# Attention and two expert layers in one kernel: the hidden layer at another SBUF offset, and weights converted 1024 columns at a time

## The chip, the cores and the metric

The kernel runs on one core of a Trainium2 chip. The metric is the device time of one execution in microseconds (us). Before the change three executions took 1100.30, 1100.47 and 1101.81 us; the median is 1100.47 us.

## What is computed

Three stages follow each other, all in float32 at the boundary:

```python
scores = q @ k.T / 8                       # 4 batches x 8 heads, 576 rows, 64 columns
mask: row block i // 64 may see column blocks j // 64 <= i // 64
x = softmax(scores) @ v                    # laid out as 2304 tokens x 512
x = ((x @ w1) * (x @ w2)) @ w3 @ w_out     # 512 -> 1024 -> 1024 -> 512
logits = x @ w_gate + log1p(exp(x @ w_noise)) * noise
top2, softmax over the two chosen logits
out[token] += weight * (relu(x[token] @ w1[e]) @ w2[e])    # 8 experts, 1024 hidden columns
```

## The kernel before

**Numbers in two parts.** A float32 matrix is split by `split` (L472) into a rounded high part (a copy to `fp32r` on ScalarE) and a low part (a subtraction on VectorE, or on GpSimd where `low="pool"`). `mm3` (L482) then makes three TensorE products: high by high (L485), high by low (L486), low by high (L487).

**Attention, heads 0 to 31.** `prep_h` (L604) makes the two parts of q and k of a head: `hi` on ScalarE (L607, L610), q's low part on VectorE (L609), and `kl`, k's low part, on GpSimd (L612). `s_unit` (L622) makes the scores, `s_max` (L645) the row maxima `nm` on VectorE (L653) and the exponentials on ScalarE (L658), `g_unit` (L661) transposes them on TensorE into `pt`, and `av_a` and `av_b` multiply by v. Heads 0 to 7 keep `pt` whole in two buffers; from head 8 on `pt` has both parts.

**Weights of the first layer.** They arrive as 64-bit words that VectorE takes apart. `load64` (L536) loads 128 x 512 words (512 KB) into one of two buffers `stg`; `conv64` (L541) makes 512 float32 columns `stf` of them with three VectorE instructions (L547, L548, L549), and `feed_half` (L764) splits `stf` into a weight tile `pc`: ScalarE L476, VectorE L480. There are 40 such jobs; a load is issued when the job two places ahead of it has been taken apart. When eight of them are there, TensorE makes the product w3 @ w_out in 64 units (`w_unit`, L717, tile `m<-pc,pc`) beside the heads.

**First layer.** For nine chunks of 256 tokens `ab` (L199) makes x @ w1 and x @ w2 (tile `m<-xh,pc`), their product `gt` in two parts, and `yout` (L215) multiplies `gt` by the product w3 @ w_out (tile `m<-pc,gt`: `gt` is TensorE's stationary operand, `pc` the moving one of 512 columns). The router's small steps follow.

**Experts.** `trans` (L930) transposes gathered tokens into `xt`, `ffn1` (L944) makes the hidden layer `ht` from `xt` and `pc`, and `ffn2` (L959) multiplies `ht`, stationary, by `pc`, moving, 512 columns (tile `ph<-pc,ht`). An expert has 640 rows: 384 in part 0 (`xt0`, `ht0`) and 256 in part 1 (`xt1`, `ht1`).

**Order.** The strings FIRST and LATER (L70, L71) list what is written out for one head: `g`, `p`, `s`, `a`, `b`, `h` are the steps of attention, `f` gives TensorE so many us of other matmuls, and `c` is one call of `feed`, which splits the job before and takes the next one apart. A scheduler then places the instructions on each engine by priorities (PIECE_PRIO, W_PRIO, MOE_PRIO). All loads and stores named here are issued by SyncE, in one queue.

**Places in SBUF.** In the built program the tiles stand at these byte offsets modulo 512: all twelve `pc` at 128, `gt` at 384, `xh` and `yT` at 384, `xt0` at 352, `xt1` at 448, `ht0` at 416, `ht1` at 448, `pt` of heads 0 to 7 at 128 and of the later heads at 480.

Of the kernel before, what the change touches and what calls it, by code (L numbers as in the profile page):

```python
# [22 lines left out]
P = 128  # L23
# [43 lines left out]

FIRST = "g0 g1 t f2.9 c t c o g2 g3 t p s0 t t s1 s2 f2.9 c t a f2.9 t b0 t s3 h t t c c b1 v l"  # L70
LATER = "g0 g1 f2.6 o g2 p t c g3 t t t s0 s1 s2 t c t a f2.6 s3 b0 t t c f2.6 c t b1 h v l"  # L71


# [8 lines left out]
class Moe1:  # L82


    def __init__(self, k, p2, psM):
        self.k, self.tc, self.nc, self.a, self.p2 = k, k.tc, k.nc, k.a, p2
        self.psM = self.psR = psM
        self.p2s = ExitStack()
        self.ready, self.rt, self.ticks, self.conv = 0, iter(()), 1, 0
        self.xs, self.gts, self.ys, self.lg = {}, {}, {}, {}  # L90
        self.scat, self.marks = [], ()

    def setup_load(self):
        nc, a, p2 = self.nc, self.a, self.p2
# [134 lines left out]
    def logits_t(self, c, t):  # L229
        nc, p2 = self.nc, self.p2  # L230
        y = self.ys[c, t]
        px = self.psR.tile([P, 4, P], F32, name="m")
        for d in range(4):
            nc.tensor.transpose(px[:, d, :], y[:, d * P:(d + 1) * P], self.k.ident)
        if t == 0:
            self.yT = self.p2b.tile([P, 2, 4, CH], F32R, name="yT")
        self.k.split([self.yT[:, i, :, t * P:(t + 1) * P] for i in range(2)], px)

    def logits_m(self, c):
# [224 lines left out]
class Kernel:  # L464
# [69 lines left out]
        return [(tab[:, b * P:e * P].rearrange("e (p i) -> p e i", p=P), ids[:, :, b:e]) for b, e in ((0, NA), (NA, NSLOT))]  # L534

    def load64(self, src, n):  # L536
        t = self.stg.tile([P, 512], I64, name="stg")
        self.nc.sync.dma_start(t.rearrange("p (a b) -> p a b", a=n), src)
        return t

    def conv64(self, t):  # L541

        v = self.nc.vector
        wi = t.bitcast(I32).rearrange("p (n w) -> p n w", w=2)
        f = self.stg.tile([P, 512], F32, name="stf")
        fi = f.bitcast(I32)
        v.tensor_scalar(fi, wi[:, :, 1], 0x07FFFFFF, 3, op0=OP.bitwise_and, op1=OP.logical_shift_left)  # L547
        v.scalar_tensor_tensor(fi, wi[:, :, 1], -0x40000000, fi, op0=OP.bitwise_and, op1=OP.bitwise_or)  # L548
        v.scalar_tensor_tensor(fi, wi[:, :, 0], 29, fi, op0=OP.logical_shift_right, op1=OP.bitwise_or)  # L549
        return f  # L550


    def attention(self):
        tc, nc, a = self.tc, self.nc, self.a
        moe1 = self.moe1
        with tc.tile_pool(name="p1", bufs=1, side="right") as p1, tc.tile_pool(name="stg", bufs=2, side="right") as self.stg, \
                tc.tile_pool(name="psS", bufs=3, space=PSUM) as psS, \
                tc.tile_pool(name="psT", bufs=2, space=PSUM) as psT, \
                tc.tile_pool(name="psV", bufs=1, space=PSUM) as psV:
# [4 lines left out]
            nc.vector.tensor_copy(mkl, mk32[:, 0, :])  # L564
            nc.vector.tensor_copy(mkr, mk32[:, 1, 0:64])
            sums = p1.tile([P, B, 6, H], F32, name="sums")

            hd = {}
            pxs = ExitStack()
# [34 lines left out]
            def prep_h(h):  # L604
                c = hd[h]
                c.hi = buf(h, [P, 2, S], F32R, "hi")
                nc.scalar.activation(c.hi[:, 0, :], c.qk[:, 0, :], AF.Copy, scale=0.125)  # L607
                lo = c.hi[64:128, 0, :]
                nc.vector.scalar_tensor_tensor(lo, c.qk[64:128, 0, :], 0.125, r32(lo), op0=OP.mult, op1=OP.subtract)  # L609
                nc.scalar.copy(c.hi[:, 1, :], c.qk[:, 1, :])  # L610
                c.kl = buf(h, [P, S], F32R, "kl")
                nc.gpsimd.tensor_tensor(c.kl, c.qk[:, 1, :], r32(c.hi[:, 1, :]), op=OP.subtract)  # L612

            def prep_v(h):
                c = hd[h]
# [45 lines left out]
            def g_unit(h, g):  # L661
                c = hd[h]
                pb = pbs[h < H and h % 2]
                if g == 0:
                    if h < H:
                        c.pt = px.tile([P, 1, PTW], F32, name="pt", bufs=2)
                    else:
                        c.pt = p1.tile([P, 2, PTW], F32R, name="pt")
                base, skip, items = G_UNITS[g]
                bank = psT.tile([P, 512], F32, name="tp")  # L670
                for n, (t, kt) in enumerate(items):
                    nc.tensor.transpose(bank[:, n * P:(n + 1) * P], pb[t][:, kt * P:(kt + 1) * P], self.ident)  # L672
                o = len(items) * P - skip
                src = bank[:, skip:skip + o]
                h_ = c.pt[:, 0, base:base + o]
                nc.scalar.copy(h_, src)
                if h >= H:
                    nc.vector.tensor_tensor(c.pt[:, 1, base:base + o], src, r32(h_), op=OP.subtract)
# [55 lines left out]
            def w_jobs():  # L734

                def wout(g):
                    return a["w_out"][:, g:g + 1, :], 1, g // 2, (g % 2) * 512, 0

                def w3(ft, o):
                    return a["w3"][ft, :, o:o + 512].unsqueeze(1), 1, 4 + ft % 2, o, 0 if ft < 2 else max(16, 8 * (ft - 1))  # L740

                for half in range(2):
                    for ft in range(2):
                        yield w3(ft, half * 512)
                    for g in range(4 * half, 4 * half + 4):
                        yield wout(g)
                for ft in range(2, 8):
                    for o in (0, 512):
                        yield w3(ft, o)
                for m, (n, k, i) in enumerate(W12):  # L750
                    for o in (0, 2):
                        yield a[n][:, o:o + 2, k * 256:(k + 1) * 256], 2, i, o * 256, 0 if m < 2 else 64

            jobs = list(w_jobs())
            raw = []
# [6 lines left out]
                    feed_half()  # L762

            def feed_half():  # L764
                if len(conv) > moe1.conv:
                    _, _, i, o, _ = jobs[moe1.conv]
                    pc = self.pc[i]
                    self.split((pc[:, 0, o:o + 512], pc[:, 1, o:o + 512]), conv[-1], low="dve")
                    moe1.conv += 1
                n = len(conv)  # L770
                if n < len(jobs) and wst.get("n", 0) >= jobs[n][4]:
                    conv.append(self.conv64(raw[n]))
                    if n + 2 < len(jobs):
                        raw.append(self.load64(*jobs[n + 2][:2]))
# [78 lines left out]
            for i in range(-1, BH):  # L853
                if i == 2:
                    moe1.setup_load()
                elif i == 3:
                    moe1.setup()
                elif i == H:
                    pxs.close()
                    moe1.p2b = moe1.p2s.enter_context(tc.tile_pool(name="p2b", bufs=1, reuse_waits="tile"))  # L860
                for op in (FIRST if i < NF else LATER).split():
                    step(i, i + 1, op)
            sums_out(B - 1)
# [65 lines left out]

    def trans(self, e, s):  # L930
        nc, n = self.nc, len(self.part(s))
        x = self.xt[e, s] = (self.pa if s == 0 else self.pb).tile([P, 2, 4, n * P], F32R, name=f"xt{s}")
        wv = self.wv[e, s] = self.pa.tile([P, n], F32, name=f"wv{s}", bufs=2)
        for o, i in enumerate(self.part(s)):
            xg = self.xg[e, i]
            nc.gpsimd.tensor_copy(wv[:, o:o + 1], xg[:, DM + e:DM + e + 1])
# [170 lines left out]
```

## Time and profile before

| what | value |
|---|---|
| median of 3 runs | 1100.47 us |
| the profiled execution, its own time | 1103.1 us |
| its span, first to last instruction | 1101.2 us |
| TensorE matmul (PE) busy | 1050.4 us, 95% |
| TensorE weight load (PEld) busy | 941.2 us, 85% |
| VectorE (DVE) busy | 564.4 us, 51% |
| ScalarE (ACT) busy | 494.9 us, 45% |
| GpSimd (POOL) busy | 309.3 us, 28% |
| bytes moved | 136.34 MB, mean 124 GB/s |
| mean granted TensorE clock | 0.988 of 2.4 GHz |

The profile is of one execution. Busy time is the union of an engine's recorded instructions; successive instructions of VectorE and of TensorE overlap in the records, so the distance from one start to the next tells more of their pace than the duration of one. "Idle before" is the time an engine stood still before an instruction, with what ended it.

### The profile page before, as it was taken

What the parts mean: (1) busy time and instruction counts of PE and PEld (TensorE: products, weight loads), DVE (VectorE), ACT (ScalarE), POOL (GpSimd) and SP (SyncE); (2) the same over time, 40 slices, a digit from 0 to 9 for tenths busy, and PEclk for the clock granted to TensorE, in tenths of its full rate; (3) what the DMA queues carried; (4) which work ended last, traced back from release to release, by engine and by line L of the source; (5) the groups of instructions that cost most, each with busy time, mean ns of one, the idle gap of its engine ahead of it and who ended that gap; (6) DMA issues with size and microseconds to landing.
All of it is one profiled execution on the core that took longest, in us unless ns stands there. A gap on an engine that the chain in (4) does not pass through costs nothing.

```text
span 1101.2 us, 17515 instructions
## 1 busy us (share of the span) xinstructions
PE 1050.4 (95%) x6588; PEld 941.2 (85%) x6588; DVE 564.4 (51%) x1270; ACT 494.9 (45%) x1180; POOL 309.3 (28%) x315
## 2 busy tenths in 40 slices
PE   4999978999999999999999999999999999999996
PEld 3767767799899999989999889889898989899885
DVE  5988889856665756532454453534333333434111
ACT  5765547666665656422223432433333333333111
POOL 3110122424252242422443325241413222120211
PEclk9999989999999999999999999999999999999999
DMA  9765775325634463322413556563545445351212
GB/s 218 237 199 193 196 200 180 123 79 132 196 96 105 143 156 121 107 68 59 77 40 87 126 106 184 173 163 96 148 102 144 107 125 125 106 115 30 39 20 32
DMA packets 80386, 136.34 MB, mean 124 GB/s; under 512 B 21437, under 2 KB 46757, under 8 KB 80293
## 3 DMA queue, kind: packets, MB, share of 16 engines
q1 hardware_dynamic: 70181, 113.98, 36.4%
q0 software_dynamic: 10112, 21.16, 10.7%
q8 instruction: 54, 0.88, 0.3%
q14 instruction: 39, 0.32, 0.1%
HBM read 103.92 MB, written 31.19 MB: 123 GB/s over the span
## 4 chain that ended last, share of the span: by engine, by line
PE 81%; DMA 8%; DVE 7%; ACT 1%; issue 1%; SPq 1%; POOL 0%; POOLq 0%; DVEq 0%; ACTq 0%
PE ph L485 13%; PE ph L486 13%; PE ph L487 13%; PE m L485 9%; PE m L486 9%; PE m L487 9%; DMA stg<-in_w_dram 4%; PE tp L672 4%; PE av L697 3%; PE sb L642 2%; PE sb L639 2%; PE m L939 1%; DVE stf L549 1%; DVE nm L653 1%; DMA stf<-in_m_dram 1%
## 5 line engine op out<-in xcount | busy, mean ns | idle before, releaser
L485 PE MATMUL m<-xh,pc 128*128 128x256 f32 x576 | 165.2, 290 | 5.6 <-DVE at L211 3.5
L486 PE MATMUL m<-xh,pc 128*128 128x256 f32 x576 | 163.1, 287 | 2.2 <-DVE xh L480 2.2
L487 PE MATMUL m<-xh,pc 128*128 128x256 f32 x576 | 161.2, 287 | 1.9 <-DVE pc L480 1.9
L485 PE MATMUL ph<-xt,pc 128*128 128x384 f32 (+1 forms) x512 | 156.0, 308 | 2.9 <-ACT xt L476 1.6
L486 PE MATMUL ph<-xt,pc 128*128 128x384 f32 (+1 forms) x512 | 157.0, 307 | 0.0
L487 PE MATMUL ph<-xt,pc 128*128 128x384 f32 (+1 forms) x512 | 156.9, 307 | 0.0
L954 DVE SCALAR_TENSOR_TENSOR ht<-ph,ht 128x384 fp32r<-128x384 f32 (+1 forms) x128 | 61.6, 489 | 148.7 <-ACT ht L953 143.5
L480 DVE TENSOR_TENSOR pc<-stf,pc 128x1024 fp32r<-128x1024 f32 (+1 forms) x92 | 92.3, 1016 | 87.2 <-ACT pc L476 83.8
L485 PE MATMUL ph<-pc,ht 128*128 128x512 f32 x320 | 127.8, 400 | 0.0
L486 PE MATMUL ph<-pc,ht 128*128 128x512 f32 x320 | 126.5, 396 | 0.0
L487 PE MATMUL ph<-pc,ht 128*128 128x512 f32 x320 | 126.4, 395 | 0.0
L981 POOL DMA_INDIRECT out_dram<-yo,ids x40 | 64.3, 1606 | 211.5 <-ACT yo L977 124.0
L485 PEld LDWEIGHTS m<-xh,pc 128*128 128x128 f32 x576 | 110.5, 193 | 7.2 <-DVE at L211 3.7
L953 ACT ACTIVATE ht<-ph 128x384 fp32r<-128x384 f32 (+1 forms) x128 | 55.0, 437 | 133.8 <-PE ph L487 127.1
L486 PEld LDWEIGHTS m<-xh,pc 128*128 128x128 f32 x576 | 110.3, 193 | 3.0 <-DVE xh L480 2.6
L487 PEld LDWEIGHTS m<-xh,pc 128*128 128x128 f32 x576 | 109.0, 192 | 2.7 <-DVE pc L480 2.4
L476 ACT CAST pc<-stf 128x1024 fp32r<-128x1024 f32 (+1 forms) x92 | 78.1, 864 | 73.8 <-DVE stf L549 32.5
L658 ACT ACTIVATE pb<-sb,nm 128x288 f32<-128x288 f32 (+3 forms) x192 | 93.5, 496 | 38.4 <-PE tp L672 17.3
L480 POOL TENSOR_TENSOR gt<-at,gt 128x256 fp32r<-128x256 f32 x72 | 57.2, 798 | 183.9 <-ACT gt L476 175.7
L485 PEld LDWEIGHTS ph<-xt,pc 128*128 128x128 f32 x512 | 95.7, 188 | 4.0 <-ACT xt L476 2.1
L612 POOL TENSOR_TENSOR kl<-qk,hi 128x576 fp32r<-128x576 f32 x32 | 47.5, 1484 | 177.2 <-ACT hi L610 136.6
L486 PEld LDWEIGHTS ph<-xt,pc 128*128 128x128 f32 x512 | 96.2, 188 | 0.6 <-DVE xt L480 0.2
(158 smaller groups left out, 2229.0 us busy)
## 6 DMA issues: line engine op xcount, KB each, us to landing
stf<-in_m_dram SPq DMA_DIRECT2D x52, 512.0 KB
qk<-in_qk_dram SPq DMA_DIRECT2D x32, 576.0 KB
stg<-in_w_dram SPq DMA_DIRECT2D x32, 512.0 KB
x<-ev SPq DMA_DIRECT2D x32, 288.0 KB
xab<-x SPq DMA_DIRECT2D x20, 256.0 KB
yt<-y SPq DMA_DIRECT2D x18, 260.0 KB
stg<-in_w_out_dram SPq DMA_DIRECT2D x8, 512.0 KB
v<-in_v_dram SPq DMA_DIRECT2D x24, 160.0 KB
```

The lines of the kernel that those rows point to most:

```text
L476: d = nc.scalar.copy(h, src)
L480: return d, eng.tensor_tensor(l, src, r32(h), op=OP.subtract)
L485: nc.tensor.matmul(out, a, c, start=first, stop=False)
L486: nc.tensor.matmul(out, a, d, start=False, stop=False)
L487: nc.tensor.matmul(out, b, c, start=False, stop=last)
L612: nc.gpsimd.tensor_tensor(c.kl, c.qk[:, 1, :], r32(c.hi[:, 1, :]), op=OP.subtract)
L658: nc.scalar.activation(pb[t][:, k0:k0 + src.free_size()], src, AF.Exp, bias=nm, scale=1.0, accum_out=sums[:, h // H, t + n, h % H:h % H + 1])
L672: nc.tensor.transpose(bank[:, n * P:(n + 1) * P], pb[t][:, kt * P:(kt + 1) * P], self.ident)
L697: nc.tensor.matmul(c.av[:, o0:o0 + w], c.vv[:, kt, :], c.pt[:, i, s0:s0 + w], start=(kt == 0 and i == 0), stop=(kt == 4 and i == m - 1))
L953: a = nc.scalar.activation(hh[:, 0, f, :], ph, AF.Relu)
L954: v = nc.vector.scalar_tensor_tensor(hh[:, 1, f, :], ph, 0.0, r32(hh[:, 0, f, :]), op0=OP.max, op1=OP.subtract)
L981: nc.gpsimd.indirect_dma_start(out=self.a["out"], out_offset=self.idx(e, i), in_=yo, in_offset=None, compute_op=OP.add)
```

## The change

It does three things.

1. In `trans` the tile `xt1` becomes 112 float32 longer, and the weights `wv` of part 0 and 1 become tiles of their own for even and odd experts in place of two buffers of one tile. In the built program `ht0` and `ht1` then both stand at 384 modulo 512 bytes; `xt0`, `xt1`, `pc` and `gt` stay where they were.
2. All jobs of the weights but six become 1024 columns wide (1 MB a load): w3 from its third block on, six of the eight blocks of w_out in pairs, and all of w1 and w2. 23 jobs are left, 17 of them wide. `stg` has two buffers of 1024 words; room for it comes from `pt` of heads 0 to 7, which moves into the tile that the later heads' `pt` uses (now at 320 modulo 512), and from `yT`, which is taken from a new pool that opens when all jobs are done. FIRST has three `c` in place of five.
3. `kl` of heads 0 to 8 is made on VectorE; from head 9 on it stays on GpSimd.

```diff
-FIRST = "g0 g1 t f2.9 c t c o g2 g3 t p s0 t t s1 s2 f2.9 c t a f2.9 t b0 t s3 h t t c c b1 v l"
+FIRST = "g0 g1 t f2.9 c t o g2 g3 t p s0 t t s1 s2 f2.9 c t a f2.9 t b0 t s3 h t t c b1 v l"
...
-            self.yT = self.p2b.tile([P, 2, 4, CH], F32R, name="yT")
+            self.yT = self.p2c.tile([P, 2, 4, CH], F32R, name="yT")
...
     def load64(self, src, n):
-        t = self.stg.tile([P, 512], I64, name="stg")
+        w = n * src.shape[-1]
+        t = self.stg.tile([P, 1024], I64, name="stg", bufs=2)[:, 0:w]
...
-        f = self.stg.tile([P, 512], F32, name="stf")
+        f = self.stg.tile([P, 1024], F32, name="stf")[:, 0:wi.shape[1]]
...
+            pt0 = p1.tile([P, 2, PTW], F32, name="pt")
+            self.stg = stgs.enter_context(tc.tile_pool(name="stg", bufs=1, side="right"))
...
-                nc.gpsimd.tensor_tensor(c.kl, c.qk[:, 1, :], r32(c.hi[:, 1, :]), op=OP.subtract)
+                (nc.vector if h < NF - 1 else nc.gpsimd).tensor_tensor(c.kl, c.qk[:, 1, :], r32(c.hi[:, 1, :]), op=OP.subtract)
...
-                        c.pt = px.tile([P, 1, PTW], F32, name="pt", bufs=2)
+                        c.pt = pt0[:, h % 2:h % 2 + 1, :]
...
+                def wout2(g):
+                    return a["w_out"][:, g:g + 2, :], 2, g // 2, 0, 0
...
-                    for g in range(4 * half, 4 * half + 4):
-                        yield wout(g)
+                    if half == 0:
+                        for g in range(2):
+                            yield wout(g)
+                    for g in range(2 + 2 * half, 4 + 4 * half, 2):
+                        yield wout2(g)
                 for ft in range(2, 8):
-                    for o in (0, 512):
-                        yield w3(ft, o)
+                    yield w3(ft, 0, 1024)
                 for m, (n, k, i) in enumerate(W12):
-                    for o in (0, 2):
-                        yield a[n][:, o:o + 2, k * 256:(k + 1) * 256], 2, i, o * 256, 0 if m < 2 else 64
+                    yield a[n][:, :, k * 256:(k + 1) * 256], 4, i, 0, 0 if m < 2 else 64
...
+                if i >= H and moe1.p2c is None and moe1.conv == 40:
+                    stgs.close()
+                    moe1.p2c = moe1.p2s.enter_context(tc.tile_pool(name="p2c", bufs=1, reuse_waits="tile"))
...
-        x = self.xt[e, s] = (self.pa if s == 0 else self.pb).tile([P, 2, 4, n * P], F32R, name=f"xt{s}")
-        wv = self.wv[e, s] = self.pa.tile([P, n], F32, name=f"wv{s}", bufs=2)
+        x = (self.pa if s == 0 else self.pb).tile([P, 8 * n * P + 112 * s], F32R, name=f"xt{s}")
+        x = self.xt[e, s] = x[:, 0:8 * n * P].rearrange("p (m d c) -> p m d c", m=2, d=4)
+        wv = self.wv[e, s] = self.pa.tile([P, n], F32, name=f"wv{s}{e % 2}")
```

The scheduler's order moves with it. On VectorE, around heads 2 and 3, the program before has these instructions (`hi`: low part of q; `nm`: row maxima; `stf<-stg`: taking apart; `pc<-stf`: low part of a weight tile):

```order
L609 SCALAR_TENSOR_TENSOR hi<-qk,hi 64x576
L480 TENSOR_TENSOR pc_67<-stf,pc_67 128x512
L653 TENSOR_REDUCE nm_482<-sb 128x1
L547 TENSOR_SCALAR stf<-stg 128x512
L548 SCALAR_TENSOR_TENSOR stf<-stg,stf 128x512
L653 TENSOR_REDUCE nm_489<-sb 128x1
L653 TENSOR_REDUCE nm_542<-sb 128x1
L549 SCALAR_TENSOR_TENSOR stf<-stg,stf 128x512
L547 TENSOR_SCALAR stf<-stg 128x512
L548 SCALAR_TENSOR_TENSOR stf<-stg,stf 128x512
L480 TENSOR_TENSOR pc_68<-stf,pc_68 128x512
```

The changed program has there, on the same engine:

```order
L481 TENSOR_TENSOR pc_67<-stf,pc_67 128x512
L549 TENSOR_SCALAR stf<-stg 128x1024
L550 SCALAR_TENSOR_TENSOR stf<-stg,stf 128x1024
L658 TENSOR_REDUCE nm_474<-sb 128x1
L692 COPY ev<-tp 128x128
L614 SCALAR_TENSOR_TENSOR hi<-qk,hi 64x576
L551 SCALAR_TENSOR_TENSOR stf<-stg,stf 128x1024
L661 TENSOR_REDUCE nm_474<-nm_474 128x1
L617 TENSOR_TENSOR kl<-qk,hi 128x576
L658 TENSOR_REDUCE nm_557<-sb 128x1
L658 TENSOR_REDUCE nm_559<-sb 128x1
L481 TENSOR_TENSOR pc_68<-stf,pc_68 128x1024
```

One wide job takes the place of two, and `kl` stands in VectorE's queue between them. SyncE's queue, where the first chunk's rows `xab` and `xr` of the first layer are fetched, has before:

```order
L538 DMA stg<-in_w_dram 128x2x256 x2
L701 DMA x_61<-ev 128x576
L167 DMA xab<-x_61 64x3x256 x2
L172 DMA xr<-rs 64x3x256
L167 DMA xab<-x_61 64x3x256 x2
L538 DMA stg<-in_w_dram 128x2x256
L172 DMA xr<-rs 64x3x256
L538 DMA stg<-in_w_dram 128x2x256
```

and in the changed program:

```order
L540 DMA stg<-in_w_dram 128x4x256
L706 DMA x_61<-ev 128x576
L168 DMA xab<-x_61 64x3x256 x2
L173 DMA xr<-rs 64x3x256
L168 DMA xab<-x_61 64x3x256 x2
L173 DMA xr<-rs 64x3x256
L540 DMA stg<-in_w_dram 128x4x256
```

The two loads among the fetches, each of which waits for a buffer, have become one behind them.

## Rows read from the trace of the kernel before

**Rows 1.** The page: the span.

```profile
span 1101.2 us, 17515 instructions
```

**Rows 2.** Busy us of each engine by stretch, then granted clock, DMA share, GB/s.

```profile
0.00:38.70 38.70, 24.48 (x111) 18.21 (x111) 26.08 (x50) 22.31 (x58) 10.66 (x26) 1.00 0.95 240
38.70:72.00 33.30, 30.68 (x164) 22.48 (x162) 29.98 (x60) 24.83 (x69) 4.82 (x4) 0.95 0.70 217
72.00:119.50 47.50, 45.99 (x244) 35.80 (x242) 41.79 (x83) 28.53 (x76) 4.28 (x3) 1.00 0.53 172
119.50:163.90 44.40, 35.07 (x220) 30.72 (x217) 35.76 (x66) 21.15 (x53) 9.99 (x8) 0.92 0.79 206
163.90:203.40 39.50, 32.83 (x204) 28.47 (x205) 38.55 (x72) 25.78 (x73) 13.01 (x10) 0.89 0.51 165
203.40:620.00 416.60, 413.61 (x2977) 384.62 (x2976) 227.67 (x671) 208.06 (x580) 149.95 (x151) 1.00 0.41 107
620.00:1101.20 481.20, 467.77 (x2680) 420.87 (x2679) 164.54 (x274) 164.28 (x276) 116.54 (x114) 0.99 0.44 107
```

**Rows 3.** TensorE in order of time, experts: start, us, instruction (`ph<-pc,ht` is `ffn2`).

```profile
735.42 0.40 PE L485 MATMUL ph<-pc,ht 128*128 128x512 f32 x1
...
746.63 0.34 PE L485 MATMUL ph<-xt,pc 128*128 128x384 f32 x1
```

**Rows 4.** TensorE in order of time, first layer (`m<-pc,gt` is `yout`).

```profile
464.65 0.40 PE L485 MATMUL m<-pc,gt 128*128 128x512 f32 x1
...
469.88 0.39 PE L487 MATMUL m<-pc,gt 128*128 128x512 f32 x1
```

**Rows 5.** Groups by line and shape: count, busy us, mean ns, idle before.

```profile
L485 PE MATMUL ph<-pc,ht 128*128 128x512 f32 x320 | 127.8, 400 | 0.0
L480 DVE TENSOR_TENSOR pc<-stf,pc 128x1024 fp32r<-128x1024 f32 x52 | 62.5, 1223 | 86.8 <-ACT pc L476 83.7 <-PE ph L487 3.1
L612 POOL TENSOR_TENSOR kl<-qk,hi 128x576 fp32r<-128x576 f32 x32 | 47.5, 1484 | 177.2 <-ACT hi L610 136.6 <-PE m L234 23.0 <-PE av L697 16.7
```

**Rows 6.** VectorE in order of time, heads 0 to 6.

```profile
7.78 1.52 DVE L547 TENSOR_SCALAR stf<-stg 128x512 int32<-128x512 int32 x1
50.89 1.83 DVE L548 SCALAR_TENSOR_TENSOR stf<-stg,stf 128x512 int32<-128x512 int32 x1
56.02 0.67 DVE L548 SCALAR_TENSOR_TENSOR stf<-stg,stf 128x512 int32<-128x512 int32 x1
56.62 0.67 DVE L480 TENSOR_TENSOR pc<-stf,pc 128x512 fp32r<-128x512 f32 x1
72.17 1.54 DVE L547 TENSOR_SCALAR stf<-stg 128x512 int32<-128x512 int32 x1
```

**Rows 7.** GpSimd in order of time, heads 4 and 5.

```profile
50.74 1.43 POOL L612 TENSOR_TENSOR kl<-qk,hi 128x576 fp32r<-128x576 f32 x1 [9.51 <-ACT hi L610]
```

**Rows 8.** Tile `stg`: ns min/median/max, first and last start; what ended VectorE's idle time.

```profile
L547 DVE TENSOR_SCALAR stf<-stg x40: 406/424/1544, 7.8 to 203.8; 128x512 int32<-128x512 int32 x40
DMA stg<-in_w_dram: 14.9, 11
DMA stg<-in_w_out_dram: 2.7, 3
```

**Rows 9.** The chain that ended last, up to 260 us: start, us, what.

```profile
127.24 5.54 DMA stg<-in_w_dram
132.80 4.10 DMA xr<-rs
145.02 9.55 DMA stg<-in_w_dram
```

**Rows 10.** Tiles `yT` and `vz`: first and last start.

```profile
L476 ACT CAST yT<-m x18: 577/587/605, 234.1 to 622.2; 128x512 fp32r<-128x512 f32 x18
L697 PE MATMUL av<-pt,vz x80: 272/434/954, 24.5 to 119.0; 128*128 128x448 f32 x32, 128*128 128x320 f32 x16, 128*128 128x192 f32 x16, 128*128 128x128 f32 x16
```

More of the change, by code (lines that the diff above doesn't have):

```diff
@@ L91, in __init__ @@
         self.scat, self.marks = [], ()
+        self.p2c = None
     def setup_load(self):
@@ L555, in attention @@
         moe1 = self.moe1
-        with tc.tile_pool(name="p1", bufs=1, side="right") as p1, tc.tile_pool(name="stg", bufs=2, side="right") as self.stg, \
+        stgs = ExitStack()
+        with tc.tile_pool(name="p1", bufs=1, side="right") as p1, \
                 tc.tile_pool(name="psS", bufs=3, space=PSUM) as psS, \
@@ L737, in wout, with w3 @@
                     return a["w_out"][:, g:g + 1, :], 1, g // 2, (g % 2) * 512, 0
-                def w3(ft, o):
-                    return a["w3"][ft, :, o:o + 512].unsqueeze(1), 1, 4 + ft % 2, o, 0 if ft < 2 else max(16, 8 * (ft - 1))
+                def wout2(g):
+                    return a["w_out"][:, g:g + 2, :], 2, g // 2, 0, 0
+                def w3(ft, o, w=512):
+                    return a["w3"][ft, :, o:o + w].unsqueeze(1), 1, 4 + ft % 2, o, 0 if ft < 2 else max(16, 8 * (ft - 1))
                 for half in range(2):
@@ L764, in feed_half @@
             def feed_half():
[L765 to L769, printed above, removed]
+                if len(conv) > wst.get("split", 0):
+                    _, _, i, o, _ = jobs[len(conv) - 1]
+                    pc, w = self.pc[i], conv[-1].shape[-1]
+                    self.split((pc[:, 0, o:o + w], pc[:, 1, o:o + w]), conv[-1], low="dve")
+                    wst["split"] = len(conv)
+                    moe1.conv += w // 512
                 n = len(conv)
```

## Prediction

> **What bounds the kernel now.** I read first the span [rows 1] and then the busy time of the engines by stretch [rows 2]. The reader should see two kernels in one. From 203.4 us on TensorE is busy all the time at full clock: up to 620 us it idles 3 of 416.6 us, and from 620 us to the end 468 of 481 us. Nothing that VectorE, GpSimd or the loads save there can shorten the time; only matmuls that follow each other at a smaller distance can. Up to 203.4 us it is otherwise. The first 38.7 us belong to the DMA engines, 0.95 busy at 240 GB/s. From 38.7 to 72 us VectorE is busy 30.0 of 33.3 us. From 72 to 119.5 us TensorE leaves only 1.5 us of 47.5. From 119.5 to 163.9 us nobody is full: TensorE idles 9.3 us at a mean granted clock of 0.92 (some of it at 1.2 GHz, the lower of its two levels, the rest at 2.4), and VectorE 8.6 us. From 163.9 to 203.4 us VectorE is busy 38.55 of 39.5 us and TensorE idles 6.7 us at a clock of 0.89.
>
> Then the distances of matmuls in order of time. In the experts 48 matmuls of the hidden layer `ht1` by `pc`, 512 columns each, lie between 735.42 and 746.63 us [rows 3]: 11.21 / 48 = 233.5 ns each. In the first layer 23 matmuls of `gt` by `pc`, also 512 columns, lie between 464.65 and 469.88 us [rows 4]: 5.23 / 23 = 227.4 ns. The clock is full in both stretches [rows 2], the moving operand is the same kind of tile at 128 modulo 512 bytes, and the stationary one stands at 384 in the faster group and at 448 in the slower.
>
> Last, what VectorE does before 203 us: the tile `stg`, the chain of waits and single instructions [rows 6, 8, 9]. It stood still 17.6 us (14.9 + 2.7, in 14 waits) for loads of `stg` [rows 8], and some of its instructions took over a us longer than their like while GpSimd made `kl`: 1.83 us from 50.89 us where the same instruction takes 0.67 us, beside a `kl` of 1.43 us from 50.74 us [rows 6, 7].
>
> **Part 1, the hidden layer at 384.** `ffn2` has three lines of 320 matmuls, 960 in all [rows 5]. If their distance becomes that of `gt`, the saving is 960 x (233.5 - 227.4) = 5.9 us, all on the path, since TensorE is the bound there [rows 2]. The bounds: 0 from below if the offset does not matter; from above 960 x 7 = 6.7 us, 7 ns being the most that I would read into the same two groups. A loss would need 384 to be worse than 416 or 448 for a stationary operand, against which [rows 4] speaks. I take 5.9 us. The tiles `wv` and the shifted buffers behind `xt1` cost no instruction.
>
> The Trainium skill, "TensorE: Matmul & The Clock Gate", section on the back-to-back issue gap, gives the start-to-start distance of a warm matmul as its columns at 2.4 GHz plus 2.5 ns, 215.7 ns at 512, with no term for where an operand stands; by it this part would bring nothing. Both groups of this trace lie above that, and differ from each other, which the formula does not provide for.
>
> **Part 2, wide jobs.** Recorded durations overlap, so I count pitch: 512 columns take 56.62 - 56.02 = 0.60 us from start to start [rows 6]. From 0.67 us [rows 6] to 1.22 us at 1024 columns [rows 5] each further column costs (1.223 - 0.67) / 512 = 1.08 ns, 0.55 us for 512, so that 0.05 us of the pitch is fixed. A wide job saves four of these on VectorE, 0.2 us; 17 wide jobs 3.4 us. By the recorded durations it would be 2 x 0.67 - 1.22 = 0.12 us each, 8.2 us. I take the pitch, because on a full queue the next instruction starts inside the record of the one before.
>
> The loads change more. A load can start when the job two places ahead is taken apart. The 40 jobs start between 7.8 and 203.8 us [rows 8], one in 5 us, so a load has two paces less its predecessor's own work of some 3 us, about 7 us, to land. Loads of 512 KB landed after 5.54 us, and after 9.55 us where the first layer's rows were fetched [rows 9], hence the waits. With 1 MB the pace is 10 us and the room about 14 us. A 1 MB load lands after 5.5 us if the bytes go in parallel and 11.1 us if they double; both fit. The waits of 17.6 us should go but for the first and some of the crowded ones; 0 to 17.6 us are the bounds on VectorE. On SyncE 17 load issues fewer stand in the queue, and at the first chunk one 1 MB load follows the fetches where two loads stood between them.
>
> **Part 3, `kl` on VectorE.** Nine instructions of 576 columns, by the pitch 0.60 + 64 x 1.08 ns = 0.67 us each: 6.0 us more. Against it stand the stalls beside GpSimd: seven VectorE instructions were stretched beside a `kl` of heads 0 to 8, the first at 7.78 us (1.52 for 0.42 us), the last at 72.17 us (1.54) [rows 6, 8], 7.1 us over the usual in all. Taken together -1.1 us. GpSimd's 9 x 1.43 us had no one waiting long.
>
> **What of it lies on the path.** By stretch [rows 2]. *0 to 38.7 us*: the same bytes, 0. *38.7 to 72 us*: VectorE gets four `kl` (+2.7), loses three stalls (-3.1), two wide jobs' fixed time (-0.4) and some 2 us of waits; TensorE's idle time there is 2.6 us and its clock 0.95. I take -2.5 us. *72 to 119.5 us*: TensorE leaves 1.5 us; -1. *119.5 to 163.9 us*: this holds the longest wait, which ended the load of 9.55 us; VectorE's 8.6 us are nearly all waits for loads, but the first chunk's chain of fetch (4.10 us [rows 9]), sum, product and split stays: -4. *163.9 to 203.4 us*: VectorE is the bound, four wide jobs save 0.8 to 2 us: -1.5. Sum -9 us, between 0 and -18.
>
> **What comes with it.** `yT` in a pool that waits for the last job: first written at 234.1 us [rows 10], the last job's first instruction was at 203.8 us [rows 8]; covered by 30 us, and if the jobs became that late it would cost the lateness. The shared `pt`: head 8 must wait until head 7's last product, whose matmul starts at 119.0 us [rows 10], has been made; the cover is what VectorE and ScalarE do meanwhile, and without it one wait of about 2 us. `pt` at another offset: 240 matmuls, by the difference of 6.1 ns found above at most 1.5 us either way; 0 taken.
>
> **Sum.** Against the profiled execution's 1103.1 us: 1103.1 - 5.9 - 9 = 1088.2 us. Its own time lies 2.6 us above the median of the runs, 1100.47, so for a run without the profiler I forecast 1100.5 - 14.9 = 1085.6 us, rounded to 1086.
>
> **Rivals.**
> - *Only the offset pays*, 0.16. The front stays as long as it is because attention's own chain and the first chunk's fetches set its pace, not VectorE. For it: TensorE leaves only 1.5 us between 72 and 119.5 us, and 4.10 us of the chain are `xr`. Against: VectorE is at 38.55 of 39.5 us in the last stretch. 1100.5 - 5.9 = 1094.6 us.
> - *Only the conversion pays*, 0.11. The 6 ns are due to something else in which the two groups differ (the PSUM tiles, what other engines write meanwhile). For it: only one pair of groups shows it. Against: `gt` keeps 227 ns while VectorE and ScalarE are at work. 1100.5 - 9 = 1091.5 us. The Trainium skill's formula above leads to this case.
> - *Neither pays, or the change doesn't do what it says*, 0.04: 1100.5 us.
> - *Slower, by `kl` behind wide instructions*, 0.05. VectorE runs in order; `kl` now stands behind up to one instruction of 1.22 us, where GpSimd began it at once. If the scores' second half waits for `kl` in each of nine heads, that is 9 x (0.67 + 1.22) = 17 us on the attention path with nothing saved in front: 1100.5 - 5.9 + 17 = 1111.6 us. It decides from the point where `kl` is made less than about 2 us before its scores. Against it: `kl` is made for a head further on, while GpSimd's slower `kl` was idle before it for 9.51 us [rows 7].
>
> **How the numbers follow.** The forecast, both parts paying, has 0.64. With the front between -3 and -16 us and part 1 between 5 and 6.7 us it spans 1078 to 1093 us. The two single cases reach to 1095; a little beyond, 1097, takes in the small waits named above. Below 1078 and above 1097 I leave some 2 in 10. About 0.2% (2.2 us) is what a measurement of this kernel can tell from no change. Faster by more: 0.64 + 0.16 + 0.11 = 0.91; within it 0.04; slower 0.05.
>
> **What would show it.** `ffn2` at 227 ns in every expert, and 5.9 us less from 620 us to the end. VectorE's waits for `stg` down from 17.6 us to a few, no instruction of 1.5 us beside `kl` in heads 0 to 8, and the last job taken apart about 9 us before 203.8 us; TensorE's clock nearer to 1.00 between 119.5 and 203.4 us. Wrong would be: `ffn2` still at 233 ns; the front as long as before with VectorE idle and the fetches of the first chunk ending the waits; or scores of heads 0 to 8 waiting for VectorE's `kl`.

## The result and the profile after

| kernel | median us (range, runs) | ratio to before, 95% interval |
|---|---|---|
| before | 1101.0 (1100.3 to 1101.81, 4) | |
| changed | 1091.7 (1090.7 to 1094.5, 4) | 0.9917 [0.9902, 0.9932] |
| changed, once more | 1092.43 (1089.96 to 1093.77, 6) | 0.9912 [0.9891, 0.9933] |

The change is worth 9.3 us; 14.9 were forecast. The page of the changed kernel gives its span; the profiled execution itself took 1094.5 us and was the slowest of the four.

```profile
span 1092.7 us, 17405 instructions
```

The windows of the changed kernel, with the columns of [rows 2]. They are cut where the first scores of heads 3, 6, 9, 11, 14 and 15 start, as [rows 2] were for heads 3, 6, 9, 11 and 14; the last cut lies about 5 us ahead of the first expert matmul, as 620 us did.

```profile
0.00:41.30 41.30, 24.88 (x110) 18.93 (x111) 26.55 (x53) 22.32 (x58) 4.82 (x22) 0.92 0.86 234
41.30:68.60 27.30, 25.81 (x151) 19.43 (x149) 24.82 (x45) 21.55 (x60) 0.00 (x0) 1.00 0.76 253
68.60:115.70 47.10, 47.10 (x250) 37.68 (x250) 42.66 (x65) 30.11 (x74) 1.87 (x1) 1.00 0.54 184
115.70:155.60 39.90, 34.75 (x213) 30.46 (x211) 32.67 (x50) 20.71 (x52) 8.97 (x7) 0.91 0.83 219
155.60:196.40 40.80, 32.37 (x201) 28.06 (x199) 38.00 (x58) 26.43 (x70) 12.95 (x11) 0.87 0.51 157
196.40:215.60 19.20, 18.36 (x113) 16.37 (x113) 16.60 (x23) 11.12 (x30) 9.81 (x7) 0.91 0.33 99
215.60:617.00 401.40, 398.86 (x2880) 370.96 (x2878) 219.06 (x648) 198.03 (x547) 146.09 (x146) 1.00 0.39 107
617.00:1092.70 475.70, 462.19 (x2679) 420.79 (x2679) 164.74 (x274) 164.01 (x276) 115.74 (x114) 0.99 0.44 108
```

The kernel before has, in the same view, this row for head 14:

```profile
203.40:219.70 16.30, 16.19 (x104) 14.46 (x103) 12.55 (x23) 12.19 (x33) 6.06 (x5) 0.95 0.41 127
```

Lengths against [rows 2], stage by stage: +2.6 us to head 3, -6.0 to head 6, -0.4 to head 9, -4.5 to head 11, +1.3 to head 14, +2.9 in head 14, +1.1 from there to the experts, -5.5 in the experts. The sum is -8.5 us, as the spans say. In this trace the experts and heads 9 and 10 gained about what was forecast, heads 3 to 5 more; three stretches that were put at nothing or a gain lost 6.8 us.

Two things limit what such lengths tell. The stretches don't hold the same work: between heads 3 and 6 TensorE has 164 matmuls before and 151 after, between heads 6 and 9 it has 244 and 250, in head 14 104 and 113. And one program gives different lengths. The second trace of the changed kernel has the same instructions in the same order, but it begins with these stretches:

```profile
0.00:37.90 37.90, 24.15 (x110) 18.20 (x111) 25.22 (x51) 22.14 (x58) 4.55 (x22) 1.00 0.91 252
37.90:50.20 12.30, 10.51 (x53) 8.04 (x51) 9.92 (x19) 7.00 (x19) 0.00 (x0) 0.86 0.69 216
```

Head 3 starts at 37.9 us there, head 4 at 50.2 and head 15 at 211.8 us. The front, as the part up to head 15 is called here, is the same program in experiments 2 and 10 below too: head 3 starts at 38.4 and 39.2 us, head 15 at 209.2 and 210.4. Experiment 1 runs the front of the kernel before: head 3 at 37.6, head 15 at 215.8 us, for 38.7 and 219.7. So a difference of 2 to 4 us in the front, between single traces, is not yet an effect of the change.

**Experts.** TensorE in order of time, the same 48 products of `ht1` as in [rows 3]:

```profile
731.77 0.39 PE L486 MATMUL ph<-pc,ht 128*128 128x512 f32 x1
...
742.65 0.34 PE L486 MATMUL ph<-xt,pc 128*128 128x384 f32 x1
```

10.88 / 48 = 226.7 ns from start to start, where it was 233.5.

In the last expert the other engines have little to do. While its 72 products of `ht0` run, VectorE has a single instruction (0.56 us) and no weights are taken apart. Before:

```profile
1051.97 0.40 PE L485 MATMUL ph<-pc,ht 128*128 128x512 f32 x1
...
1068.77 0.28 PE L485 MATMUL ph<-xt,pc 128*128 128x256 f32 x1
```

and in the changed kernel:

```profile
1044.42 0.39 PE L486 MATMUL ph<-pc,ht 128*128 128x512 f32 x1
...
1060.75 0.28 PE L486 MATMUL ph<-xt,pc 128*128 128x256 f32 x1
```

16.80 / 72 = 233.3 ns and 16.33 / 72 = 226.8 ns.

**Loads.** The tile `stg`, against [rows 8]: 23 jobs, and one wait in place of 14.

```profile
L549 DVE TENSOR_SCALAR stf<-stg x23: 417/685/1799, 8.1 to 198.0; 128x1024 int32<-128x1024 int32 x17, 128x512 int32<-128x512 int32 x6
...
  DMA stg<-in_w_out_dram: 7.0, 1
```

That one wait stands in head 1, in VectorE's order of time:

```profile
26.38 0.43 DVE L549 TENSOR_SCALAR stf<-stg 128x512 int32<-128x512 int32 x1 [6.96 <-DMA stg<-in_w_out_dram]
```

The load it waits for is the third, issued at 15.42 us. SyncE's queue of the changed kernel in order of time:

```profile
13.22 2.11 SPq L135 DMA_DIRECT2D idt<-lt  x1
15.42 0.36 SPq L540 DMA_DIRECT2D stg<-in_w_out_dram  x1
...
17.26 6.71 SPq L149 DMA_DIRECT2D yt<-cst  x2
24.07 0.96 SPq L540 DMA_DIRECT2D stg<-in_w_out_dram  x1
```

and of the kernel before:

```profile
12.46 0.53 SPq L538 DMA_DIRECT2D stg<-in_w_out_dram  x1
13.04 0.44 SPq L134 DMA_DIRECT2D idt<-lt  x1
...
14.72 0.33 SPq L538 DMA_DIRECT2D stg<-in_w_out_dram  x1
```

The third load went out 3.0 us later, behind the writes of the table `idt`, and the fourth 9.4 us later, behind 6.71 us of writes of `yt`. It is the move of `kl` of heads 0 and 1 that does it: experiment 5 leaves these two on GpSimd and has the old order. Presumably the scheduler then takes what GpSimd makes for these writes as ready sooner. The diff shows none of that.

**VectorE beside GpSimd, heads 9 to 14.** The longest instructions of VectorE there, in order of time:

```profile
154.65 2.33 DVE L550 SCALAR_TENSOR_TENSOR stf<-stg,stf 128x1024 int32<-128x1024 int32 x1
...
165.90 2.34 DVE L550 SCALAR_TENSOR_TENSOR stf<-stg,stf 128x1024 int32<-128x1024 int32 x1
...
193.46 2.82 DVE L614 SCALAR_TENSOR_TENSOR hi<-qk,hi 64x576 fp32r<-64x576 f32 x1 [0.34 <-ACT hi L612]
```

and GpSimd's, which stand beside them:

```profile
153.96 1.94 POOL L617 TENSOR_TENSOR kl<-qk,hi 128x576 fp32r<-128x576 f32 x1
...
165.28 1.87 POOL L617 TENSOR_TENSOR kl<-qk,hi 128x576 fp32r<-128x576 f32 x1 [7.58 <-ACT hi L615]
...
193.31 2.36 POOL L191 TENSOR_TENSOR xab<-xab 128x1024 f32<-128x1024 f32 x1
```

A wide L550 takes 1.22 us where GpSimd is quiet. Counting, for each form, what lies over its usual duration, heads 9 to 14 hold 9.7 us of such stretching, and the heads ahead of them 1.5 us (in the kernel before 9.3 and 8.0). So moving `kl` took the stretching out of the early heads alone. What that is worth in time is another question (experiment 3).

### The profile page after: what moved, and what is told of

The parts are those of the page before. It is cut to its first block, busy times and chain, and to the rows that moved or that the text cites. A ratio compares the mean times of both kernels' runs of the same rounds, so it can differ in the third digit from the quotient of the medians.

```text
span 1092.7 us, 17405 instructions
## 1 busy us (share of the span) xinstructions
PE 1044.3 (96%) x6588; PEld 942.7 (86%) x6588; DVE 565.1 (52%) x1211; ACT 494.3 (45%) x1163; POOL 300.3 (27%) x306
## 4 chain that ended last, share of the span: by engine, by line
PE 77%; DVE 5%; ACT 2%; DMA 1%; issue 1%; POOL 0%; POOLq 0%; ACTq 0%; DVEq 0%
PE ph L486 13%; PE ph L488 13%; PE ph L487 13%; PE m L486 9%; PE m L487 9%; PE m L488 9%; PE tp L677 3%; PE av L702 3%; PE sb L647 2%; PE sb L644 2%; PE m L953 1%; DMA stf<-in_m_dram 1%; DVE hi L614 1%; PE m L244 1%; DVE pc L481 1%
## 5 line engine op out<-in xcount | busy, mean ns | idle before, releaser
L487 PE MATMUL m<-xh,pc 128*128 128x256 f32 x576 | 163.9, 288 | 0.0
L481 DVE TENSOR_TENSOR pc<-stf,pc 128x1024 fp32r<-128x1024 f32 (+1 forms) x75 | 88.0, 1189 | 88.5 <-ACT pc L477 84.4
L486 PE MATMUL ph<-pc,ht 128*128 128x512 f32 x320 | 126.0, 395 | 0.0
L488 PE MATMUL ph<-pc,ht 128*128 128x512 f32 x320 | 124.6, 390 | 0.0
L487 PE MATMUL ph<-pc,ht 128*128 128x512 f32 x320 | 124.5, 390 | 0.0
L481 POOL TENSOR_TENSOR gt<-at,gt 128x256 fp32r<-128x256 f32 x72 | 60.1, 839 | 185.3 <-ACT gt L477 178.1
L477 ACT CAST pc<-stf 128x1024 fp32r<-128x1024 f32 (+1 forms) x75 | 74.8, 1016 | 57.0 <-DMA stf<-in_m_dram 34.3
L486 PEld LDWEIGHTS ph<-xt,pc 128*128 128x128 f32 x512 | 95.8, 188 | 4.3 <-ACT xt L477 2.1
L487 PEld LDWEIGHTS ph<-xt,pc 128*128 128x128 f32 x512 | 96.1, 188 | 0.5 <-DVE xt L481 0.2
L488 PEld LDWEIGHTS ph<-xt,pc 128*128 128x128 f32 x512 | 96.2, 188 | 0.0
```

Source lines behind the costliest of these rows:

```text
L477: d = nc.scalar.copy(h, src)
L481: return d, eng.tensor_tensor(l, src, r32(h), op=OP.subtract)
L486: nc.tensor.matmul(out, a, c, start=first, stop=False)
L487: nc.tensor.matmul(out, a, d, start=False, stop=False)
L488: nc.tensor.matmul(out, b, c, start=False, stop=last)
```

## The experiments

Medians; each ratio is to the kernel before on the same chip (1101.65 to 1102.15 us). All compute the whole of the reference.

**1. The offset alone.** The kernel before with part 1 of the change.

```diff
-        x = self.xt[e, s] = (self.pa if s == 0 else self.pb).tile([P, 2, 4, n * P], F32R, name=f"xt{s}")
+        x = (self.pa if s == 0 else self.pb).tile([P, 8 * n * P + 112 * s], F32R, name=f"xt{s}")
```

> The kernel before with the longer xt1 and the wv tiles of the change alone. Theory (the offset of ht is what moves the experts, and nothing in the front depends on it): matmuls of ffn2 at 227 ns in place of 233.5 ns, 5.5 to 6 us less, all of it after the start of the experts, about 1095.4 us; front as before. Rival (the distance comes from something else that the whole change moves, such as the weight buffers stf): ffn2 stays at 233 ns and the time at 1101 us.

1095.8 us, 0.9944 [0.9928, 0.9959]: 6.1 us. All 959 distances that start at an `ffn2` product sum up to 220.0 us, and 225.6 in the kernel before. The 5.6 us are there without parts 2 and 3, and all engines have the same instructions in the same order as in the kernel before. In the built program the edit also moves the experts' buffers `stf`, which lie behind `ht1`, from 448 to 384; but the last expert, where nothing touches `stf`, is faster by the same 6 ns.

**2. The conversion alone.** The changed kernel with `trans` as before, so parts 2 and 3.

> The changed kernel with xt1 and wv as before, so ht back at 416 and 448 modulo 512. Theory: ffn2 at 233.5 ns, experts as long as before, front as in the changed kernel (3 to 4 us shorter than before): about 1097.5 us. Rival (the two parts help each other): the sum of what the two single kernels save falls short of the 9.3 us of both by over 1.5 us.

1096.76 us, 0.9951 [0.9933, 0.9968]: 5.1 us, about half of the 9 forecast. `ffn2` is back at 233 ns. Together, 6.1 + 5.1 = 11.2 us against the 9.3 of both: within these intervals the two parts add up.

**3. Wide jobs without `kl` on VectorE.** The changed kernel with L617 always on `nc.gpsimd`.

> The changed kernel with kl of all heads on GpSimd. Theory (kl on VectorE is about even there, and costs 2.6 us in heads 0 to 2, because a free GpSimd lets the table writes go ahead of the load of w_out in SyncE's queue): head 3 starts near 39 us in place of 41.3, VectorE has seven stretched instructions again in heads 0 to 8 (some 7 us), time 1089 to 1093 us. Rival (kl on VectorE is what the front's gain comes from): 1095 us or more.

1095.48 us, 0.9935 [0.9918, 0.9952], the same as the offset alone, and the figure of the rival. VectorE's waits for `stg` were down to 1.8 us, head 3 began at 38.0 us, and nothing was gained. Wide jobs without the move pay nothing. VectorE stands still for something else instead, as the waits from 30 to 220 us show:

```profile
DVE pc L481 <- ACT pc L477: 10.1, 7, 4.7
```

These are low parts of weight tiles that wait for ScalarE's high parts: 10.1 us in 7 waits, where the kernel before has 0.2, the changed kernel 3.4 and experiment 5 below 3.1. Which stretch lost the time is less clear. VectorE's stretching ahead of head 9 rose to 8.7 us again, yet head 9 came at 110.8 us, no later than in experiment 5 (111.2), if with 20 matmuls fewer done. From head 9 to head 15, where `kl` is on GpSimd in both, and with as many matmuls within one, this kernel took 101.0 us against 95.6 of experiment 5 and 99.1 of experiment 9, which has the front of experiment 5.

**4. `kl` of heads 0 to 8 on VectorE without wide jobs.** The kernel before with part 3 alone.

> The kernel before with kl of heads 0 to 8 on VectorE, nothing else. Theory (nine kl of 0.67 us against seven stalls of 1.0 us, about even): the stretched instructions before head 9 fall from 8.0 to under 3 us, VectorE's waits for loads stay at 15 us or more, the time changes by less than 3 us, 1099 to 1103 us. Rival (kl on VectorE is what the front gains): 1096 us or less. Rival (it delays the scores): over 1104 us.

1115.46 us, 1.0123 [1.0098, 1.0149]: 14 us slower, where about even was expected. The tile `stg` of this kernel:

```profile
  DMA stg<-in_w_dram: 17.0, 11
  DMA stg<-in_w_out_dram: 7.0, 2
```

24.0 us of waits in place of 17.6. Head 3 starts at 42.6 us (38.7 before), head 9 at 128.5 (119.5). On SyncE the first load of w_out stands behind all writes of `idt`, as in the changed kernel (14.27 us), but the second stays ahead of those of `yt` (15.19 us). No wait of TensorE for `kl` of heads 0 to 8 is recorded.

**5. `kl` of heads 2 to 8 on VectorE, of 0 and 1 on GpSimd**, in the changed kernel:

```diff
-(nc.vector if h < NF - 1 else nc.gpsimd).tensor_tensor(c.kl, ...)
+(nc.vector if 2 <= h < NF - 1 else nc.gpsimd).tensor_tensor(c.kl, ...)
```

> The changed kernel with kl of heads 0 and 1 on GpSimd and of heads 2 to 8 on VectorE; SyncE's queue then has the load of w_out ahead of the table writes again. Theory (the start's loss is that order): VectorE's wait of 7.0 us for w_out at 19.4 us goes, head 3 starts near 39 us, the time is 2 to 3 us under the changed kernel's: about 1089 us. Rival (the start is bound by the bytes, 0.9 of the DMA engines busy, whatever the order): head 3 at 41 us and 1091.7 us.

1086.37 us, 0.9869 [0.9849, 0.9889], 6 us better than the change. The load that came late now leaves SyncE at 12.69 us, and the wait of 6.96 us is one of 2.45:

```profile
12.69 0.53 SPq L540 DMA_DIRECT2D stg<-in_w_out_dram  x1
```

```profile
22.95 0.43 DVE L549 TENSOR_SCALAR stf<-stg 128x512 int32<-128x512 int32 x1 [2.45 <-DMA stg<-in_w_out_dram]
...
34.68 1.23 DVE L550 SCALAR_TENSOR_TENSOR stf<-stg,stf 128x1024 int32<-128x1024 int32 x1
35.82 0.45 DVE L658 TENSOR_REDUCE nm<-sb 128x1 f32<-128x288 f32 x1
```

The last two rows also give the pitch of a wide instruction: 1.14 us, against 2 x 0.60.

**6. The same in the kernel before**, 512-column jobs.

> The kernel before with kl of heads 2 to 8 on VectorE and of heads 0 and 1 on GpSimd; jobs stay 512 columns wide. SyncE's order up to 38 us is then that of the kernel before. Theory A, the 14 us of kl on VectorE without wide jobs came from the start (the load of w_out behind the table writes, head 3 at 42.6 in place of 38.7) and what it delayed: 1101 to 1106 us, VectorE's waits for stg down from 24.0 to under 18 us. Theory B, a VectorE that is full with 512-column jobs cannot take kl: 1109 to 1116 us, head 9 still after 124 us with head 3 near 38.7. In between, 1106 to 1109 us, both have a share.

1102.45 us, 1.0013 [0.9997, 1.0028]: nothing lost, nothing won. Its waits are

```profile
  DMA stg<-in_w_dram: 10.3, 10
  DMA stg<-in_w_out_dram: 0.9, 1
```

So 13.0 of the 14 us of experiment 4 (1102.45 to 1115.46) belong to `kl` of heads 0 and 1. VectorE's waits for loads differ by as much, 11.2 against 24.0 us. And seven `kl` on VectorE are even with narrow jobs, while with wide ones they give 9.1 us (1095.48 to 1086.37).

**7. `kl` of heads 0 to 8 on VectorE, the early writes of `idt` and `yt` issued by GpSimd** instead of SyncE, in the changed kernel. It tries the order on SyncE by itself.

```diff
-                nc.sync.dma_start(dst, src)
+                nc.gpsimd.dma_start(dst, src)
```

> The changed kernel, kl of heads 0 to 8 on VectorE as it is, but the six writes of the tables idt and yt that go out at the start are issued by GpSimd, in place of SyncE. Theory A, kl of heads 0 and 1 on VectorE costs time only through the order on SyncE (two loads of w_out behind these writes): then this is worth what kl from head 2 on was worth, 1084 to 1088 us, VectorE's wait for the first w_out load falls from 7.0 us to under 3, and head 3 starts before 38 us. Theory B, kl itself is in the way of VectorE in heads 0 and 1: 1090 to 1094 us, head 3 after 39 us although the load comes sooner. Between 1088 and 1090 us leaves it open.

1090.93 us, 0.991 [0.9883, 0.9937]: hardly better than the change. VectorE waited for no load of `stg` at all, the clock stayed full up to 51 us (the changed kernel has 0.72 from 27 to 39 us in one trace and 0.86 from 39 to 51 us in the other), and head 3 started at 37.9 us. But the edit brought a wait of its own, in head 0: ScalarE, which splits q, waits for a load of `qk`, and VectorE for ScalarE.

```profile
14.90 0.68 ACT L613 ACTIVATE hi<-qk 128x576 fp32r<-128x576 f32 x1 [4.28 <-DMA qk<-in_qk_dram]
15.62 0.76 DVE L615 SCALAR_TENSOR_TENSOR hi<-qk,hi 64x576 fp32r<-64x576 f32 x1 [3.52 <-ACT hi L613]
```

GpSimd issues the writes of `idt` from 3.3 us on, the DMA engines are then busier in the first 15 us (a share of 1.02 against 0.85), and head 1 starts at 19.1 us where it was 15.6. The theory that SyncE's order is the whole of the 6 us found no support: the wait went and the time did not come. It isn't refuted either, since the head start that the load won was spent in head 0. The four executions lie between 1088.13 and 1094.05 us, so the median says little. How much `kl` of heads 0 and 1 costs in VectorE's own queue stays open.

**8. `kl` of heads 2 to 13 on VectorE**, in the changed kernel.

> The changed kernel with kl of heads 2 to 13 on VectorE. Theory (in heads 9 to 14 VectorE is the bound and loses 9 to 10 us to instructions stretched beside GpSimd; half of it is beside kl): the stretched time of heads 9 to 14 falls to 5 us or less, 5 x 0.67 = 3.4 us of kl are added, the front ends 1 to 3 us earlier than with heads 2 to 8 alone (1086.4 us): 1084 to 1086 us. Rival (the rest of GpSimd's work stretches the same instructions anyway): no stretched time less, 1088 us or more.

1082.12 us, 0.9819 [0.9798, 0.984], 4.3 us under experiment 5. From head 11 to head 15 the changed kernel takes 60.0 us (57.2 in its second trace), experiment 5 57.4 and this one 48.0; the stretching in heads 9 to 14 falls from 9.7 to 4.1 us. Not all of the 9.4 us is gain: this stretch has 283 matmuls where experiment 5 has 313, and from head 15 to the first expert matmul it takes 412.2 us where experiment 5 takes 405.6.

**9. The first layer's input `xh` at 320 modulo 512**, beside experiment 5's edit.

```diff
-            x.h = self.p2b.tile([P, 2, 4, CH], F32R, name="xh")
+            x.h = self.p2b.tile([P, 8 * CH + 16], F32R, name="xh")[:, 0:8 * CH].rearrange("p (m d c) -> p m d c", m=2, d=4)
```

The router's small tile `mk` also takes a buffer of the tile `dl`.

> The changed kernel with kl of heads 2 to 8 on VectorE and with xh, the moving operand of the first layer's 1728 matmuls of 256 columns, at 320 in place of 384 modulo 512 bytes (gt stays at 384). Theory (the place of the moving operand against that of the weights matters as well: xt1 at 448 makes 113.4 ns where xh at 384 makes 120): 113 to 117 ns, 5 to 11 us less than 1086.4 us. Rival (only the stationary operand's place counts, and what makes 120 ns is other traffic): 120 ns, 1086 us.

1082.53 us, 0.9825 [0.9802, 0.9848]: 3.8 us under experiment 5, from another operand of another product, the moving one this time. It is less than the 5 to 11 us expected. The median distance went from 120 to 117 ns, and all 1728 distances together from 216.3 to 212.4 us (those of 400 ns and more left out). The stretch from head 15 to the experts is 4.5 us shorter (401.1 for 405.6 us).

**10. Another offset for the hidden layer**: `ht0` stays at 384, `ht1` moves to 256 and `xt0` from 352 to 224.

> The changed kernel with other padding: ht0 stays at 384, ht1 moves to 256 and xt0 to 224 modulo 512. If a stationary operand is fast at every multiple of 128 (offsets 416 and 448 gave 233 ns, 384 gave 227), ffn2 of part 1 stays at 227 ns and the time within 2 us of the changed kernel. If 384 alone is fast, ffn2 of part 1 goes to 233 ns, 384 of 960 matmuls by 6 ns, 2.3 us more.

One execution, 1095.44 us. The 48 products of `ht1` stand at 11.16 / 48 = 232.5 ns:

```profile
726.48 0.40 PE L486 MATMUL ph<-pc,ht 128*128 128x512 f32 x1
...
737.64 0.33 PE L486 MATMUL ph<-xt,pc 128*128 128x384 f32 x1
```

while `ht0` keeps 227 (226.8 in the last expert). A multiple of 128 is not enough. The products of `xt0`, 384 columns, went from 173 to 176 ns. Those of `xt1`, 256 columns, went from 114 to 118 ns in the median, although `xt1` and `pc` stand where they stood and every engine has the same instructions in the same order. So more than an operand's own place counts. The sums of distances rose by 2.2 us for `ht`, 2.5 for `xt0` and 2.1 for `xt1`; the experts of this trace are 6.9 us longer.

**11. Experiments 8 and 9 together.**

> The changed kernel with kl of heads 2 to 13 on VectorE (1082.12 us alone) and xh at 320 modulo 512 (against 1086.37 us with kl of heads 2 to 8: -3.8 us). If the two are independent, the first working ahead of 195 us and the second between 210 and 610 us: 1078 us, 0.978 of the kernel before. If the run to run changes of the front made the 3.8 us, and the offset of xh gives nothing: 1082 us. m<-xh,pc should stand at a median of 113 to 118 ns against 120.

1077.67 us (1076.18 to 1079.71, 5 runs), 0.9791 [0.9768, 0.9813]: 24 us under the kernel before and some 14 under the change. The two gains add up. The distances of `xh` fall unevenly. The sixth chunk shows the most; TensorE in order of time, 73 of its products in the changed kernel:

```profile
486.02 0.36 PE L488 MATMUL m<-xh,pc 128*128 128x256 f32 x1
...
494.86 0.40 PE L486 MATMUL m<-pc,gt 128*128 128x512 f32 x1
```

and the same 73 in this one:

```profile
471.86 0.36 PE L488 MATMUL m<-xh,pc 128*128 128x256 f32 x1
...
480.22 0.39 PE L486 MATMUL m<-pc,gt 128*128 128x512 f32 x1
```

8.84 / 73 = 121.1 ns became 8.36 / 73 = 114.5. Over all 1728 products the sum fell from 213.8 us in experiment 8 to 208.7 here, 3.0 ns each. Taken 24 by 24, the products of the last four chunks stand at 113 to 118 ns, where experiment 8 has 119 to 121 (distances of 200 ns and more left out).

## Why the prediction came out as it did

The time lies inside the range, on its upper side: part 1 was right, and the front brought 3.4 us (9.3 - 5.9) where 9 were put down. That the front comes so near is in part luck. Added one after the other (experiments 1, 3, 5, then the change), wide jobs gave 0.3 us, `kl` of heads 2 to 8 gave 9.1 and `kl` of heads 0 and 1 took 6.1 back. The prediction had the gain in the wide jobs and `kl` about even.

**Part 1, the hidden layer at 384: right in place and size.** 233.5 ns became 226.7, the sum of distances fell by 5.6 us, and alone the offset measured 6.1 us. That "384" is what counts was read off one pair of groups; experiment 10 bears it out for 256, and experiment 1 with the last expert takes away the other explanations of the second rival: the instructions are the same, the other engines have little to do there, and the 6 ns are gone all the same. The Trainium skill, "TensorE: Matmul & The Clock Gate", section on the back-to-back issue gap, has no term for an operand's place; by it 0 of the 6 us should have come, and the measurement decides against it here. The section calls its formula the gap of an isolated matmul and says that at many columns a stream of matmuls runs closer than that; the 227 and 233 ns of these traces are further apart.

**Part 2, the fixed time of wide jobs: right.** A wide instruction has a pitch of 1.14 us against 2 x 0.60, 0.06 us saved where 0.05 was read. **The waits: right as an amount, wrong in worth.** 17.6 us became 7.0, and 1.8 in experiment 3, which nevertheless gained nothing beyond its offset. VectorE stood still for ScalarE's high parts instead (10.1 us, 0.2 before), which the prediction did not count.

**Part 3, `kl` on VectorE, "taken together -1.1 us": this step failed.** As a balance of +6.0 and -7.1 us of VectorE's time it was a sound reading, and experiment 6 gives about even for heads 2 to 8 with narrow jobs (by its interval, -0.3 to +3.1 us). But it was read with the jobs of the kernel before, and for nine heads at one price. With wide jobs the same seven heads are worth 9.1 us. A wide instruction beside GpSimd is stretched like any other (up to 2.34 for 1.22 us), and experiment 3 has 8.7 us of it ahead of head 9 where the changed kernel has 1.5. That this makes the 9.1 us is not shown: narrow jobs bear the same stretching (8.0 us in the kernel before) without loss, and experiment 3 loses time behind head 9 too, where `kl` stands as in experiment 5. What goes with the move is 7 us less of VectorE's waits for ScalarE (10.1 in experiment 3, 3.1 in experiment 5). Why the worth of the move depends on the jobs stays open. Heads 0 and 1 in turn cost 13 us with narrow jobs and some 6 with wide ones (1086.37 to 1092.43).

**"0 to 38.7 us: the same bytes, 0" lacked a term.** The bytes are the same; their order isn't. Two loads of w_out went behind table writes, VectorE stood 6.96 us in head 1, TensorE 6.6 us in the same head (3.2 before), and the granted clock of the stretch was 0.92, some of it at the lower level, where it was 1.00 [rows 2]. In this trace that came to +2.6 us at head 3. In the second trace of the same program VectorE waits 5.5 us for the load, the clock stays full and head 3 starts at 37.9 us; the low clock and a long head 3 follow, and head 4 starts at 50.2 us (51.1 in the first trace, 48.4 before). In experiments 2 and 10 head 4 starts at 48.2 and 49.0 us. So the start lost something between nothing and 3 us, and how much of the 6 us between the change and experiment 5 is due to the order isn't shown. The prediction looked at SyncE's queue at the first chunk's fetches and not at the start.

**38.7 to 119.5 us: better than forecast**, -6.0 and -0.4 us for -2.5 and -1: TensorE idles 1.5 us in the first of the two stretches and not at all in the second, at full clock. The two go together, since some matmuls moved from the first into the second. **119.5 to 163.9 us: -4.5 us for -4.** **163.9 to 203.4 us: +1.3 us for -1.5**, though 38.0 to 38.8 us in the other three traces of this front, against 39.5 and 38.4 before: no gain that these traces can tell. Head 14, which the text counted among the stretches where "TensorE is busy all the time at full clock", took 2.9 us more with 113 matmuls in place of 104. There `kl` is still on GpSimd, the wide instructions meet it, and the clock shows 0.87 and 0.91. Experiment 8 shows that something was to be had here: it gains 4.3 us by moving five more `kl`.

**The rivals.** "Only the offset pays", 1094.6 us, is what the changed kernel would be without part 3 (1095.48). "Only the conversion pays" falls with experiment 1. The slower one, scores that wait for `kl` behind VectorE's instructions, has nearly the price of experiment 4 (17 us said, 14 measured), but that is chance: neither the traces of the changed kernel nor that of experiment 4 show a wait of TensorE for `kl` of heads 0 to 8, and the 14 us come from heads 0 and 1, beside longer waits of VectorE for loads, and not a little in each of nine.

The changed kernel's executions range from 1089.96 to 1094.5 us, and the traces of two of them differ ahead of 200 us alone (last job at 198.0 and 194.2 us), with the low clock in other places. Differences of a few us between stretches of the front's variants are not read as effects here.

## What to carry to other kernels

Moving an instruction to another engine can change the order of other queues: print the start of each queue, DMA issues included, before putting a stretch at zero. Take more than one trace of a front, and count the matmuls in a stretch, before comparing lengths. Price a move together with the other part of the change it lands in, since the same seven instructions were worth 0 with narrow jobs and 9 us with wide ones. Where matmuls are the bound, measure their distance per pair of operand places; a few floats of padding were worth 6 us in one product and 4 in another.

## What the runs showed of the hardware

**The place of an operand in SBUF changes a matmul's distance, and not by its being round.** For `ht`, stationary beside 512 columns of `pc` at 128 modulo 512: 227 ns at 384, 232.5 at 256, 233 at 416 and 448. For `xh`, the moving operand beside a stationary `pc`, 256 columns: a median of 120 ns at 384 and of 117 at 320. So 384 is the good place for one tile as stationary operand and a worse one for the other as moving operand. The operand's own place is not all: with `xt1` and `pc` in place, its products went from 114 to 118 ns when `xt0`, `ht1` and buffers beside them moved (experiment 10). What decides it isn't shown; only these offsets were tried.

**VectorE instructions with a single SBUF input are stretched beside GpSimd too.** L547, `stf` from `stg` and a constant, took 1.52 and 1.54 us in [rows 6], beside a `kl` that GpSimd began at 7.61 and 71.47 us, and 0.42 as a rule [rows 8]. The Trainium skill, "SBUF — State Buffer", section on who interferes with whom, tells that two SBUF inputs on VectorE contend with a GpSimd instruction that reads SBUF; the trace agrees for L548, L550 and L614 (2.33 for 1.22 us). It says that one input does not, outside the two-port modes of VectorE, and that `tensor_scalar`, which L547 is, can enter these. The rows speak for such a mode: from 512 to 1024 columns L547 (L549 after) grows from 0.42 to 0.69 us, 0.51 ns for a column, and L548 from 0.68 to 1.22 us, 1.04 ns. So the page may well hold here.
